# Grouping the filler work between the weighting steps of an attention and convolution kernel

## The chip, the core and the metric

The kernel runs on one core of a Trainium2 chip. The metric is the device time of one launch in microseconds (us); the time of a kernel is the median of several runs. Four engines compute: PE (TensorE, matrix multiplication into the PSUM accumulators), VectorE (DVE), ScalarE (ACT) and GpSimd (POOL). SyncE (SP) and POOL issue the DMA transfers.

## The reference

Two independent computations share one launch, and their outputs stand side by side, 640 columns each.

- A: `x` (2048 positions, 640 columns) goes through one projection to q, k and v with 32 heads of 20 columns. Each position attends to 8 earlier ones, at distances 0, 2, ... 14: `logits = q.k * scale`, softmax over the 8, `o = sum of weight * v`, and `o @ wo` is the output.
- B: for each of 640 channels a kernel `K` of length 2048 is generated from 192 complex exponentials, `u` is convolved with it by Fourier transforms, and `u * Dskip` is added.

## The kernel before

The change lies in the last stage, from about 353 us of the profiled execution on. By then all transforms of B are done but the last half of the inverse one, and the logits of A are made. What is left is done in one interleaved stream.

**The weighting (`av_step`, L600 to L623).** The 2048 positions lie as four quarters of 512 on the 128 partitions (quarter and head), so that v is a tile of 20 columns by 512 positions. For each of the 8 distances `w`, VectorE multiplies a stretch of v by the attention weights (L606, one instruction), and PE adds the product into PSUM with 16 small matmuls by an identity (32x32 tiles, tile `ps_o`), 8 for the first two quarters and 8 for the others. The products go through a ring of 6 buffers. After `w == 7` the sum is copied out of PSUM to `o` in two copies (L620, L622). Both engines go through six blocks, each of 8 steps:

- the first block: positions 0 to 255 of each quarter, columns 0 to 7 (products of 2048 columns)
- A: positions 0 to 127, columns 8 to 19 (1536)
- B: positions 128 to 255, columns 8 to 19 (1536)
- C: positions 256 to 383, columns 0 to 15 (2048)
- D: positions 256 to 511, columns 16 to 19 (1024)
- E: positions 384 to 511, columns 0 to 15 (2048)

A block takes two of three double PSUM buffers, so the second half of a block's first step waits until one copy of the block before is done. `between` is called in the middle of that step.

**The filler.** Between the steps PE does two other kinds of work:

- *Inverse parts* (`Inverse.part`, 24 of them): 12 or 8 matmuls (`ps_ib`) for 3 or 2 rows of the inverse transform, and one ScalarE copy to `ysb` (L680). Behind every third part, 8 rows are complete and SP issues four stores (L683). Six parts at a time read one of four `Z` tiles, which are loaded beforehand: the third (parts 12 to 17) and the fourth (18 to 23) in pieces during blocks A, B and C (`LOADS`, L667), the third by SP alone.
- *Output pieces* (`out_piece`, 32 of them): 5 matmuls with `wo` (`ps_op`) for half the columns of 128 positions, and a copy to `ob` (L638; for half of the last eight on VectorE, L636). Behind every second piece the 128 positions are stored. Eight pieces become possible each time that `o` is complete for a quarter of the positions: after A, B, D and E.

Both kinds, the softmax sums `ps_s` and small corrections share one pool of two single PSUM banks, so a piece waits until the piece but one before it has been copied out.

**What sets the order.** `in_order` makes matmuls, ScalarE copies and the instructions passed to `VV` keep the order of the program on their engine; other VectorE instructions may be moved by the scheduler. `fill(some, n)` takes the next n pieces from the list `parts` or `rest` and issues them. In the kernel before, one piece is issued behind nearly every step:

```
piece = lambda: fill(parts if done in (0, 2) or (done, w) == (1, 0) else rest)
att.av_step(i0, ni, j0, nj, w, done == 3, piece if w == 0 else lambda: None)
```

For positions 256 to 511 the softmax is finished during this stage: maxima and exponentials in the first block, the sums (`ps_s`) ahead of block B, and in `softmax_b` their reciprocal (L578) and the weights `atp` (L582), written behind step 3 of block B.

Of the kernel before, what the change touches and what calls it, by code (L numbers as in the profile page):

```python
# [10 lines left out]
A = mybir.AluOpType  # L11
ACT = mybir.ActivationFunctionType
AX = mybir.AxisListType
bf16 = mybir.dt.bfloat16
# [392 lines left out]
class Attention:  # L407
# [161 lines left out]
    def sums(self, hf):  # L569
        self.ps_s = self.one("ps_s")[:, 0:256]  # L570
        for w in range(W):
            self.MM(self.ps_s, lhsT=self.ident[:], rhs=self.lsb[hf][:, w], start=(w == 0), stop=(w == W - 1))

    def softmax_b(self, hf):
        nc, lsb = self.nc, self.lsb[hf]
        r = self.ta.tile([128, 256], bf16, name="recip", tag="TA0")
        with nc.allow_low_precision("weights are bf16 in the reference"):
            nc.vector.reciprocal(out=r[:], in_=self.ps_s)  # L578
        if hf == 0:
            self.AP_ = self.ta.tile([128, 4, 2048], bf16, name="atp", tag="R1")  # L580
        self.at[hf] = self.AP_[:, hf].rearrange("p (w i) -> p w i", w=W)
        nc.vector.tensor_tensor(out=self.at[hf], in0=lsb, in1=r[:].unsqueeze(1).to_broadcast([128, W, 256]), op=A.mult)  # L582

    def open_out(self, a2):
        nc = self.nc
# [103 lines left out]
def body(tc, ctx, pools, prm, B_u, B_Dskip, Sd, Zd, UDd, A_x, A_wqkv, A_wo, out_a, out_b):  # L689
    nc = tc.nc  # L690
# [13 lines left out]
    with tc.tile_pool(name="prep_b", bufs=1) as pb, tc.tile_pool(name="prep_c", bufs=1) as pc, tc.tile_pool(name="prep_a", bufs=1) as pa, tc.tile_pool(name="psum_p", bufs=2, space=bass.MemoryType.PSUM) as psp:  # L704
        pools.update(prep_a=pa, prep_b=pb, prep_c=pc)
        B, fill = partB_prep(tc, dict(pools, psum=psp), prm)
# [21 lines left out]
    att = Attention(tc, pools, A_x, A_wqkv, A_wo, out_a, psk, psg)  # L728
# [102 lines left out]
    for w in range(W):  # L831
        if w >= 2:
            att.products(1, w)
        att.logits(1, w)
        if w == 2:
            att.softmax_b(0)
        att.proj_v(2 * w)
        if w == 4:
            att.v_halo(0, 8)
# [3 lines left out]
    parts = inv.parts()  # L843
    rest = []

    def fill(some, n=1):
        for f in some[0:n]:
            f()
        del some[0:n]

    for w in range(W):
        if w < 4:
            att.proj_v1(16 + w)
        if w in (1, 4):
            att.v_halo(*((8, 8) if w == 1 else (16, 4)))
        if w >= 5:
            fill(parts)
        if w == 0:
            att.open_out(a2)
        att.av_step(0, 256, 0, 2, w)  # L860
        if w == 1:
            att.softmax_a(1)
        elif w == 3:
            att.exponentials(1)
    LOADS = {(d, w + 2 * (qr == 3)): (qr, c) for c, (d, w) in enumerate(((0, 0), (0, 4), (1, 0), (1, 4), (None, 0))) for qr in (2, 3)}
    for i0, ni, j0, nj, done in ((0, 128, 2, 3, 0), (128, 128, 2, 3, 1), (256, 128, 0, 4, None), (256, 256, 4, 1, 2), (384, 128, 0, 4, 3)):
        if done == 1:
            att.sums(1)
        for w in range(W):
            piece = lambda: fill(parts if done in (0, 2) or (done, w) == (1, 0) else rest)  # L870
            att.av_step(i0, ni, j0, nj, w, done == 3, piece if w == 0 else lambda: None)
            if done == 1 and w == 3:
                att.softmax_b(1)
            if (done, w) in LOADS:
                qr, c = LOADS[done, w]
                inv.load(qr, c, c + 1)
            if w > 0:
                piece()
            if done == 3 and w % 2 == 0:
                fill(parts)  # L880
        if done is not None:
            rest += att.out_proj(done, done == 3)
    for f in parts + rest:
# [4 lines left out]
def kernel(  # L888
# [28 lines left out]
    Zd = dpool.tile([NCH, 128, 4096], bf16, name="Zdram")  # L917
    UDd = dpool.tile([NCH, 128, 2048], bf16, name="UDdram")
    body(tc, ctx, pools, prm, B_u, B_Dskip, Sd, Zd, UDd, A_x, A_wqkv, A_wo, out_a, out_b)


# [28 lines left out]
```

## Time and profile before

| what | us |
|---|---|
| median of 3 runs | 425.13 (423.94 to 426.79) |
| the profiled execution | 420.77 |
| its span, first to last instruction | 419.0 |
| PE busy | 341.1 |
| VectorE busy | 382.7 |
| ScalarE busy | 310.5 |
| GpSimd busy | 47.9 |

The span is what the views of the trace divide up; the 1.8 us by which the execution is longer lie around it. Times in the views are counted from the start of the span. The mean granted clock of PE is 0.955 of full speed. PE's busy time is that of pipelined matmuls with modelled ends, so the time from the start of one group to the start of the next is the better measure of what it costs. In a timeline each row gives the start, the length, the engine, the line and operation, output and inputs, the number of merged instructions and, in brackets, how long the engine idled just before and what ended it. Nearly all matmuls of the last stage show L426, the helper that keeps them in order, so they are told apart by their tiles.

### The profile page before, as it was taken

What the parts mean: (1) busy time and instruction counts of PE and PEld (TensorE: products, weight loads), DVE (VectorE), ACT (ScalarE), POOL (GpSimd) and SP (SyncE); (2) the same over time, 40 slices, a digit from 0 to 9 for tenths busy, and PEclk for the clock granted to TensorE, in tenths of its full rate; (3) what the DMA queues carried; (4) which work ended last, traced back from release to release, by engine and by line L of the source; (5) the groups of instructions that cost most, each with busy time, mean ns of one, the idle gap of its engine ahead of it and who ended that gap; (6) DMA issues with size and microseconds to landing.
All of it is one profiled execution on the core that took longest, in us unless ns stands there. A gap on an engine that the chain in (4) does not pass through costs nothing.

```text
span 419.0 us, 17105 instructions
## 1 busy us (share of the span) xinstructions
PE 341.1 (81%) x7757; PEld 227.0 (54%) x7757; DVE 382.7 (91%) x381; ACT 310.5 (74%) x571; POOL 47.9 (11%) x85
## 2 busy tenths in 40 slices
PE   2375678989886887778868688999899999799996
PEld 1133463866864567455754557455555676444444
DVE  7999999999997999999999988994986899899762
ACT  3989996889999899979999492533667645754752
POOL 7540000000000000000000000170000300502110
PEclk9997598999899899989999899999999999969999
DMA  5599002164233403334029990440040292897544
GB/s 144 171 228 171 3 2 96 60 231 102 103 129 127 102 5 127 129 128 102 28 104 295 185 256 9 157 167 2 3 102 0 85 207 81 221 237 214 156 127 127
DMA packets 45129, 51.57 MB, mean 123 GB/s; under 512 B 31376, under 2 KB 38992, under 8 KB 42368
## 3 DMA queue, kind: packets, MB, share of 16 engines
q1 hardware_dynamic: 41520, 41.40, 36.7%
q0 software_dynamic: 3392, 8.95, 7.2%
q8 instruction: 61, 1.00, 1.0%
q10 hardware_dynamic: 144, 0.12, 0.1%
q14 instruction: 12, 0.10, 0.1%
HBM read 28.01 MB, written 18.35 MB: 111 GB/s over the span
## 4 chain that ended last, share of the span: by engine, by line
PE 33%; DVE 23%; ACT 19%; DMA 11%; issue 7%; SPq 6%; DVEq 0%; ACTq 0%
DVE Y L312 9%; DMA P<-Sdram 5%; ACT A L342 5%; ACT R L224 5%; PE ps_k L327 4%; PE ps_q L495 4%; PE ps_k L477 4%; PE ps_v L508 4%; PE ps_op L426 4%; DVE X L278 3%; ACT Sg L348 3%; PE ps_o L426 2%; DMA U<-in_B_u_dram 2%; DVE P L362 2%; PE ps_l L548 2%
## 5 line engine op out<-in xcount | busy, mean ns | idle before, releaser
L312 DVE TENSOR_TENSOR Y<-F,G 128x3072 bf16<-128x3072 bf16 x60 | 102.9, 1757 | 0.0
L327 PE MATMUL ps_k<-Y,X 64*32 64x64 bf16 (+1 forms) x3840 | 81.5, 237 | 20.5 <-DVE Y L312 14.5
L327 PEld LDWEIGHTS <-X 64*32 64x32 bf16 (+1 forms) x3840 | 62.2, 115 | 46.7 <-issue 32.8
L224 ACT ACTIVATE R<-LPC 128x192 bf16<-128x192 f32 x225 | 59.6, 358 | 0.1
L249 PE MATMUL ps_ph<-LPC 128*128 128x512 bf16 x100 | 32.2, 424 | 13.2 <-DMA LPC<-lo 6.2
L348 ACT CAST Sg<-ps_f 128x1024 bf16<-128x1024 f32 x40 | 37.7, 1025 | 6.1 <-PE ps_f L347 6.0
L342 ACT CAST A<-ps_f 128x1024 bf16<-128x1024 f32 x40 | 38.0, 1040 | 2.1 <-PE ps_f L341 2.0
L347 PE MATMUL ps_f<-A,T 128*128 128x128 bf16 x320 | 23.8, 235 | 16.0 <-ACT A L342 14.2
L278 DVE TENSOR_TENSOR X<-R,TX 128x1536 bf16<-128x1536 bf16 x40 | 36.5, 958 | 0.0
L261 ACT ACTIVATE TA<-ps_ph 128x1024 bf16<-128x1024 int16 (+1 forms) x40 | 30.4, 828 | 6.1 <-PE ps_ph L249 3.6
L606 DVE TENSOR_TENSOR prod<-v,atp 128x2048 bf16<-128x2048 bf16 (+2 forms) x32 | 30.8, 1018 | 2.4 <-PE ps_o L426 1.5
L347 PEld LDWEIGHTS <-T 128*128 128x128 bf16 x320 | 21.7, 106 | 17.8 <-issue 16.7
L261 ACT ACTIVATE TX<-ps_ph 128x1024 bf16<-128x1024 int16 (+1 forms) x40 | 29.6, 839 | 1.1 <-PE ps_ph L253 1.1
L537 DVE TENSOR_TENSOR prod<-qT,kT 128x1024 bf16<-128x1024 bf16 (+1 forms) x16 | 23.0, 1483 | 4.7 <-ACT qT L496 4.7
L362 DVE TENSOR_TENSOR P<-P,Sg 128x4096 bf16<-128x4096 bf16 x10 | 22.8, 2290 | 4.6 <-DMA P<-Sdram 2.6
L426 PE MATMUL ps_op<-wo,o 128*128 128x320 bf16 x160 | 26.3, 301 | 0.1
L638 ACT CAST ob<-ps_op 128x320 bf16<-128x320 f32 x28 | 12.0, 429 | 16.9 <-PE ps_op L426 15.6
L378 PE MATMUL ps_ia<-EA,P 128*128 128x128 bf16 x320 | 21.5, 220 | 2.9 <-DVE P L362 2.8
L328 ACT CAST Ksb<-ps_k 128x512 bf16<-128x512 f32 x20 | 11.7, 601 | 16.1 <-PE ps_k L327 16.0
L495 PE MATMUL ps_q<-xT,wkq 128*128 128x512 bf16 x100 | 22.6, 379 | 0.0
L477 PE MATMUL ps_k<-xT,wkq 128*128 128x512 bf16 x100 | 22.4, 379 | 0.0
L379 ACT CAST Z<-ps_ia 128x1024 bf16<-128x1024 f32 x20 | 19.4, 1014 | 3.7 <-PE ps_ia L378 3.7
(133 smaller groups left out, 601.7 us busy)
## 6 DMA issues: line engine op xcount, KB each, us to landing
Sdram<-Sg SPq DMA_DIRECT2D x5, 1024.0 KB
P<-Sdram SPq DMA_DIRECT2D x5, 1024.0 KB
P<-Sdram SPq DMA_DIRECT2D x10, 512.0 KB
Zdram<-Z SPq DMA_DIRECT2D x5, 1024.0 KB
Z<-Zdram SPq DMA_DIRECT2D x30, 128.0 KB
U<-in_B_u_dram SPq DMA_DIRECT2D x4, 640.0 KB
UDdram<-UD SPq DMA_DIRECT2D x10, 256.0 KB
out_dram<-ysb SPq DMA_DIRECT2D x32, 80.0 KB
```

The lines of the kernel that those rows point to most:

```text
L224: last = nc.scalar.activation(out=R[:, :, e, :], in_=src, func=ACT.Exp, scale=m)
L249: MM(full[:, 16 * gi:16 * gi + 16], lhsT=L[b][:, 0:128], rhs=C, start=(i == 0), stop=(i == len(ops) - 1))
L261: last = nc.scalar.activation(out=dst[:, q0:q0 + nq, 0:32, :].rearrange("p q e f -> p e q f"), in_=words.rearrange("p (e q f) -> p e q f", ...
L278: TT = lambda o, a, b, op: V.tensor_tensor(out=o, in0=a, in1=b, op=op)
L312: nc.vector.tensor_tensor(out=Y[:].rearrange("p q (b a) f -> p q b a f", a=8), in0=fa, in1=gb, op=A.mult)
L327: MM(ps[32 * g:32 * g + 32, t], lhsT=X[hb, q, 2 - k, :, f], rhs=Ys[k][hb, q, :, f], start=(t == 0 and n == 0), stop=(n == 5), tile_positio ...
L342: nc.scalar.copy(out=A1[:, :, 32 * b:32 * b + 32].rearrange("p k (j g) -> p k j g", g=4), in_=ps[:].rearrange("p j k g -> p k j g"))
L347: last = MM(ps[:, kk], lhsT=C["T2"][:, 8 * b + kk, :], rhs=A1[:, 8 * b + kk, :], start=(kk % 4 == 0), stop=True, skip_group_check=True)
L348: nc.scalar.copy(out=Sg[:, :, 8 * b:8 * b + 8, :], in_=ps[:].rearrange("p k (j g) -> p j k g", g=4))
L426: self.MM = lambda *a, **k: late(self.nc.tensor.matmul(*a, **k))
L477: MM(ps[:, i], lhsT=self.wk[:, kt, 128 * ct:128 * ct + 128], rhs=self.x4[:, kt, 2 * i:2 * i + 2, 256 * hf:256 * hf + 256], start=(kt == 0) ...
L495: MM(ps[:, i], lhsT=self.wq[:, kt, 128 * ct:128 * ct + 128], rhs=self.x4[:, kt, 2 * i:2 * i + 2, 256 * hf:256 * hf + 256], start=(kt == 0) ...
```

## The change

The filler is issued in groups, written out per block as what goes `inside` the first step and what goes `behind` which step. Mostly these are two pieces behind every second step; around the softmax sums of block B they are single. In the first block two parts behind step 6 stand for one each ahead of steps 5, 6 and 7. The number of parts or output pieces per block changes a little: first block 3 parts to 2; B 1 part and 7 output pieces to 2 and 6; D 8 parts to 6 parts and 2 output pieces; E 4 parts and 8 output pieces to 6 and 6, and one more output piece is left for behind E. The reciprocal becomes a method of its own, kept in order, and is called behind step 1 of block B; the weights `atp` are kept in order too and are written behind step 4.

```diff
+    def reciprocals(self):
+        self.r = self.ta.tile([128, 256], bf16, name="recip", tag="TA0")
+        with self.nc.allow_low_precision("weights are bf16 in the reference"):
+            self.VV(self.nc.vector.reciprocal(out=self.r[:], in_=self.ps_s))
+
     def softmax_b(self, hf):
-        nc, lsb = self.nc, self.lsb[hf]
-        r = self.ta.tile([128, 256], bf16, name="recip", tag="TA0")
-        with nc.allow_low_precision("weights are bf16 in the reference"):
-            nc.vector.reciprocal(out=r[:], in_=self.ps_s)
+        nc, lsb, r = self.nc, self.lsb[hf], self.r
...
-        nc.vector.tensor_tensor(out=self.at[hf], in0=lsb, in1=r[:].unsqueeze(1).to_broadcast([128, W, 256]), op=A.mult)
+        self.VV(nc.vector.tensor_tensor(out=self.at[hf], in0=lsb, in1=r[:].unsqueeze(1).to_broadcast([128, W, 256]), op=A.mult))
...
-        if w >= 5:
-            fill(parts)
         if w == 0:
             att.open_out(a2)
         att.av_step(0, 256, 0, 2, w)
+        if w == 6:
+            fill(parts, 2)
...
-    for i0, ni, j0, nj, done in ((0, 128, 2, 3, 0), (128, 128, 2, 3, 1), (256, 128, 0, 4, None), (256, 256, 4, 1, 2), (384, 128, 0, 4, 3)):
+    for i0, ni, j0, nj, done, inside, behind in (
+            (0, 128, 2, 3, 0, (parts, 2), {2: (parts, 2), 4: (parts, 2), 6: (parts, 2)}),
+            (128, 128, 2, 3, 1, (parts, 1), {1: (parts, 1), 2: (rest, 1), 3: (rest, 1), 4: (rest, 2), 6: (rest, 2)}),
+            (256, 128, 0, 4, None, (rest, 2), {2: (rest, 2), 4: (rest, 2), 6: (rest, 2)}),
+            (256, 256, 4, 1, 2, (rest, 2), {2: (parts, 2), 4: (parts, 2), 6: (parts, 2)}),
+            (384, 128, 0, 4, 3, (parts, 2), {2: (rest, 2), 3: (parts, 2), 4: (rest, 2), 5: (parts, 2), 6: (rest, 2)})):
...
-            piece = lambda: fill(parts if done in (0, 2) or (done, w) == (1, 0) else rest)
-            att.av_step(i0, ni, j0, nj, w, done == 3, piece if w == 0 else lambda: None)
-            if done == 1 and w == 3:
+            att.av_step(i0, ni, j0, nj, w, done == 3, (lambda: fill(*inside)) if w == 0 else lambda: None)
+            if done == 1 and w == 1:
+                att.reciprocals()
+            if done == 1 and w == 4:
                 att.softmax_b(1)
...
-            if w > 0:
-                piece()
-            if done == 3 and w % 2 == 0:
-                fill(parts)
+            if w in behind:
+                fill(*behind[w])
```

For the first half of the positions `reciprocals` is called just ahead of `softmax_b(0)`, where nothing is kept in order yet.

More of the change, by code (lines that the diff above doesn't have):

```diff
@@ L869, in body @@
         for w in range(W):
-            piece = lambda: fill(parts if done in (0, 2) or (done, w) == (1, 0) else rest)
-            att.av_step(i0, ni, j0, nj, w, done == 3, piece if w == 0 else lambda: None)
-            if done == 1 and w == 3:
+            att.av_step(i0, ni, j0, nj, w, done == 3, (lambda: fill(*inside)) if w == 0 else lambda: None)
+            if done == 1 and w == 1:
+                att.reciprocals()
+            if done == 1 and w == 4:
                 att.softmax_b(1)
```

## The prediction

> **What bounds the kernel now.** First the busy time of each engine by block, from the windows of the trace. The rows are the first block, A, B, C, D, E and the rest; the columns are the stretch, its length, busy time (instructions) of PE, its weight loads, DVE, ACT and POOL, the granted clock, the DMA share and GB/s.
>
> ```profile
> 353.53:363.75 10.22, 8.89 (x254) 4.63 (x252) 9.17 (x12) 6.54 (x11) 3.45 (x7) 1.00 0.73 206
> 363.75:373.74 9.99, 8.40 (x241) 3.90 (x217) 9.99 (x12) 7.46 (x13) 2.70 (x5) 0.75 1.08 253
> 373.74:382.79 9.05, 9.05 (x174) 4.12 (x173) 9.05 (x9) 3.55 (x8) 1.41 (x3) 0.90 0.71 190
> 382.79:392.15 9.36, 9.36 (x170) 4.35 (x169) 8.42 (x11) 4.71 (x11) 2.16 (x5) 1.00 0.77 240
> 392.15:398.00 5.85, 4.96 (x219) 2.66 (x218) 4.36 (x6) 5.16 (x11) 0.27 (x1) 1.00 0.31 90
> 398.00:407.89 9.89, 9.89 (x206) 4.67 (x204) 6.13 (x6) 5.66 (x14) 1.63 (x3) 1.00 0.53 136
> 407.89:419.00 11.11, 7.47 (x65) 4.76 (x50) 3.19 (x5) 3.65 (x8) 1.08 (x2) 1.00 0.38 120
> ```
>
> VectorE is full in A and B (9.99 of 9.99, 9.05 of 9.05) and has room in D and E (4.36 of 5.85, 6.13 of 9.89). PE is full in B, C and E; only D has a hole. So VectorE paces the start, PE the end. Next, PE's timeline, the rows with idle time from A on (in brackets), and with them the row that ends E:
>
> ```profile
> 365.06 0.52 PE L426 MATMUL ps_o<-prod,ident 32*32 32x384 bf16 x24 [0.65 <-ACT o L622]
> ...
> 366.44 0.32 PE L426 MATMUL ps_ib<-Z,HB 96*32 96x160 bf16 x8 [0.23 <-ACT ysb L680]
> ...
> 369.07 0.54 PE L426 MATMUL ps_o<-atp,ident 32*32 32x384 bf16 x14 [0.64 <-issue]
> ...
> 393.06 0.39 PE L426 MATMUL ps_ib<-Z,HB 96*32 96x160 bf16 x12 [0.61 <-DMA Z<-UDdram]
> ...
> 396.90 0.39 PE L426 MATMUL ps_ib<-Z,HB 96*32 96x160 bf16 x12 [0.28 <-ACT ysb L680]
> ...
> 407.89 7.52 PE L426 MATMUL ps_op<-wo,o 128*128 128x320 bf16 x50
> ```
>
> The wait of 0.61 in D is for the third `Z` tile. The chain of waits (start, length, what) shows what stands behind it, SP issuing stores and loads one after the other from 378.94 on until the last lands:
>
> ```profile
> 378.94 0.28 SPq L683
> ...
> 388.97 0.54 SPq L667
> ...
> 389.56 3.42 DMA Z<-UDdram
> 392.97 0.09 issue
> 393.06 0.39 PE ps_ib L426 x12
> ```
>
> So PE's lateness before D is partly free: whoever reaches the third tile's first part early waits for 392.97. What counts is the PE work that is left behind that landing.
>
> **The change part by part.**
>
> *The reciprocal* costs and gains nothing: in the two kernels as built VectorE's instructions stand in one and the same order, with the reciprocal behind step 5 of B.
>
> ```profile
> 371.92 1.89 PE L426 MATMUL ps_s<-lsb,ident 128*128 128x256 bf16 x8
> 373.74 0.52 PE L426 MATMUL ps_o<-prod,ident 32*32 32x384 bf16 x8
> 373.87 1.75 DVE L578 RECIPROCAL recip<-ps_s 128x256 bf16<-128x256 f32 x1
> ```
>
> The sums end at 373.81 and the reciprocal starts at 373.87: there is no room. But one inverse part fewer stands ahead of the sums now (10 instead of 11), so they come no later. If they did, VectorE would wait as long, in front of B's step 6; the price is bounded by what PE then still has in its ring.
>
> *First block and A.* VectorE's instructions and PE's A steps are the same. The part of 8 matmuls that completes the first 8 rows moves from ahead of step 7 to the middle of A's first step, and its ScalarE copy from before the two copies of `o` to behind them (first row: a group of such copies, count, then busy us, mean ns of one and idle time):
>
> ```profile
> L680 ACT CAST ysb<-ps_ib 128x320 bf16<-128x320 f32 x8 | 3.4, 427 | 2.7 <-PE ps_ib L426 2.5
> 362.42 1.65 ACT L680 CAST ysb<-ps_ib 128x480 bf16<-128x480 f32 x3
> 364.00 1.93 ACT L622 CAST o<-ps_o 128x1024 bf16<-128x1024 f32 x2
> ```
>
> The copies of `o` start up to 0.43 earlier, the 427 ns of that copy, and PE has two parts instead of one to fill the 0.65. Against this the pairs in A find their two banks still being copied. I take the sum of A as zero for the end, since the landing above covers it; without that cover it is worth between -1.5 (0.65, 0.23 and 0.64 gone) and +1.
>
> The first `ysb` store now starts about 1.8 later (behind 1.93 of `o`, less what moved ahead), and SP, in order, has most of its `Z` loads behind it. In the built order one load has moved ahead of it, and the stores of the third and fourth group of rows have moved behind 1 and 3 loads. SP's rows and waits here:
>
> ```profile
> 364.09 1.84 SPq L683 DMA_DIRECT2D out_dram<-ysb  x4
> ...
> SPq L683 <- ACT ysb L680: 3.9, 1, 3.9
> SPq L667 <- DMA Z<-Zdram: 0.9, 1, 0.9
> SPq L683 <- DMA Z<-Zdram: 0.5, 1, 0.5
> ```
>
> SP stood still for 3.9 ahead of 364.09, then twice for transfers in flight (0.9 and 0.5), in a stretch whose DMA share is 1.08. A later start is partly taken up there. The landing shifts by -0.5 to +1.8; I take 0.
>
> *B and C.* B has one output piece less, one part more. A pair of output pieces against two single ones:
>
> ```profile
> 385.62 0.85 PE L426 MATMUL ps_op<-wo,o 128*128 128x320 bf16 x5
> 386.40 0.43 PE L426 MATMUL ps_o<-prod,ident 32*32 32x512 bf16 x16
> ```
>
> A piece takes 386.40 - 385.62 = 0.78. In the row of 50 at 407.89 ten pieces one after another take 7.52, or 0.75 each. So each pair saves about 0.04. [...] These rows show no more than that. B and C change by -0.5 in PE time, which the landing covers too.
>
> *D.* At its first step two output pieces (1.53) stand where one part stood, and the first part on the third tile comes behind step 2 instead of in the middle of step 0. It needs the tile 1.53 + 2.5 steps later; a step of D is 394.38 - 394.12 = 0.26:
>
> ```profile
> 393.80 0.39 PE L426 MATMUL ps_ib<-Z,HB 96*32 96x160 bf16 x12
> 394.12 0.33 PE L426 MATMUL ps_o<-prod,ident 32*32 32x256 bf16 x16
> 394.38 0.32 PE L426 MATMUL ps_ib<-Z,HB 96*32 96x160 bf16 x8
> ```
>
> That is 2.2 later. PE came to it at about 392.45 before; it would now come at about 394.6, or up to 1.5 sooner by the gains in A, B and C. So the 0.61 goes, and the landing has between 0 and 1.6 of slack.
>
> *D and E behind the landing.* Before, PE took from 393.06 to 407.89 = 14.83: 12 parts, 7.5 steps of D, 8 of E and 7 output pieces (the eighth stands behind E's last step). After, there are 12 parts, 5 steps of D, 8 of E and 6 output pieces. That is 2.5 x 0.26 = 0.65 and 0.78 less. With three pairs of output pieces (0.12) and the 0.28 of 396.90 gone, it is 1.83 less. New waits stand against it. A pair needs both banks at once, while ScalarE copies in order:
>
> ```profile
> 391.48 1.93 ACT L622 CAST o<-ps_o 128x1024 bf16<-128x1024 f32 x2
> ...
> 395.33 1.52 ACT L680 CAST ysb<-ps_ib 128x480 bf16<-128x480 f32 x3 [0.15 <-PE ps_ib L426]
> ...
> 397.80 1.08 ACT L622 CAST o<-ps_o 128x512 bf16<-128x512 f32 x2
> ```
>
> At E's first step the copy of D's `o` (half of 1.08) comes behind a part's copy (1.52 / 3 = 0.51), and two parts (0.32 each, 394.12 - 393.80) cover 0.64 of it: about 0.2 is left. Two steps on, the pair of output pieces needs the banks of those two parts, copied behind all of the 1.08: about 0.2 again. In D the pairs of parts come every 0.26 x 2 + 0.64 = 1.16, and ScalarE needs 1.02 for two: it keeps up, barely. New waits: 0.4 to 2.6 (the upper end if each of the six pairs of parts in D and E waits one 0.43). I take 0.9, nearer to the rows that I can follow.
>
> *Behind E* nothing changes: in both kernels two old output pieces and then the eight last ones follow E's last step.
>
> **The sum:** -1.83 + 0.9 = -0.93 behind the landing, 0 at the landing, 0 for the rest. The profiled execution goes from 420.77 to 419.8 (span 418.0). The median of the runs shown stands 4.36 above that execution, so on the median's scale it is 425.13 - 0.93 = 424.2.
>
> **The rivals.**
>
> *No bound moves* (the regrouping does nothing): the gains are small against 425, and the new waits may equal 1.83. Time 425.1.
>
> *SP is the bound, and slower:* the first store is 1.8 late, nothing is taken up, and the third tile lands at 394.8. From a landing later than 392.97 + 0.93 = 393.9 the change loses; at 1.8 it is +0.87, 426.0. For it: SP issues without a break from 378.94 to 390. Against it: the load that moved ahead, and the 0.9 and 0.5.
>
> [...]
>
> *The clock.* PE's clock falls to half in A:
>
> ```profile
> 368.00:369.00 1.00, 0.43 (x14) 0.09 (x3) 1.00 (x2) 0.70 (x2) 0.00 (x0) 0.86 1.15 298
> 369.00:370.00 1.00, 0.93 (x38) 0.35 (x37) 1.00 (x2) 0.00 (x0) 0.00 (x0) 0.50 1.18 287
> ...
> 375.00:376.00 1.00, 1.00 (x29) 0.42 (x5) 1.00 (x2) 0.12 (x1) 0.00 (x0) 0.73 0.72 199
> 324.97 1.03 PE L572 MATMUL ps_s<-ql,ident 128*128 128x256 bf16 x8 [0.24 <-ACT ql L567]
> ```
>
> It lasts from about 368.7 to 375.5 (0.86 and 0.73 are means of a full and a half part). The sums take 1.89 in it and 1.03 at 324.97, at full clock. If such a stretch of 6.8 fell into E, where nothing covers it, half of it would be lost: +3.4, 427.6. If it went away, A and B would gain about 2, and the landing would cover most of that: 423. [...]
>
> *More than forecast:* the third tile lands up to 0.5 sooner, nothing waits at the banks, 0.4 is left of the new waits: 425.13 - 1.83 + 0.4 - 0.5 = 423.2; with the idle rows of A gone and the landing sooner still, 421.5.
>
> **How the numbers follow.** Chances: forecast (423.4 to 424.8) 0.40; no bound moves 0.16; SP 0.12; banks 0.10; clock 0.08; more than forecast 0.14. The predicted time is that of the likeliest, 424.2. The range takes in the clock's 427.6 above and the last case's 421.5 below; with some 0.5 on each side for the spread of the runs shown (423.94 to 426.79) it is 421.0 to 428.0. A per cent is 4.25, which is about what a measurement of this kernel can tell from no change. No term worked out here reaches it alone: the largest is the clock's 3.4. Faster by over 1% asks for the last case together with the clock's gain, or for a cause that no row shows: 0.11, out of the last case and the clock's. Slower by over 1% asks for two of the slower cases at once (the clock with the banks or with SP), or again for an unseen cause: 0.11, out of those three. Within 1% is 0.78.
>
> **What would show it.** Right: in D no idle time of PE for `Z`, or one of under 0.3; the stretch from the landing to the end of E about 13.9 instead of 14.83; the waits of `ps_ib` and `ps_op` for ScalarE's copies some 0.9 more in D and E; the ten pieces behind E as long as before; VectorE without a wait in A and B. Wrong: a landing of the third tile beyond 394; waits for `ysb` copies at every pair; a half-clock stretch in D or E; a fall of the chain back to VectorE, with PE waiting for products.

## The result and the profile after

The changed kernel takes 420.83 us (median of 22 executions, 417.56 to 426.42) against 424.02 for the kernel before on the same chips (22 executions, 419.34 to 427.72). The ratio is 0.9944, with a 95% interval of 0.9916 to 0.9971: 2.4 us faster, between 1.2 and 3.6. It leaves out the slow executions, those over 1.5% above the fastest of their kernel, and so it is not the quotient of the two medians. The forecast was 0.93 faster.

The profile that came with the result is of an execution with a low clock (0.911, span 423.6), so the kernel before is compared with a second profile of the same changed kernel (span 416.6, clock 0.950); the first one is read further down for what it alone shows.

The windows by block of that second profile, with the same columns as those of before: first block, A, B, C, D, E, rest. Each window begins at the first matmul of its block. The first window of before begins 1.18 ahead of that matmul (354.71), so its first block takes 9.04 counted this way.

```profile
353.74:362.14 8.40, 7.20 (x224) 3.98 (x228) 7.32 (x9) 5.02 (x10) 2.82 (x5) 1.00 0.69 188
362.14:372.30 10.16, 8.18 (x272) 4.39 (x256) 10.16 (x13) 7.40 (x14) 3.31 (x7) 0.83 0.96 242
372.30:381.92 9.62, 8.23 (x159) 4.01 (x143) 9.62 (x10) 3.14 (x8) 1.13 (x2) 0.82 0.69 184
381.92:390.29 8.37, 8.37 (x184) 4.55 (x168) 7.73 (x10) 4.62 (x11) 2.17 (x4) 1.00 0.86 261
390.29:395.79 5.50, 5.13 (x218) 3.01 (x202) 4.13 (x5) 5.10 (x10) 1.08 (x2) 1.00 0.47 162
395.79:405.56 9.77, 9.34 (x238) 5.11 (x229) 6.93 (x7) 6.62 (x16) 1.08 (x2) 1.00 0.60 146
405.56:416.60 11.04, 7.46 (x66) 4.78 (x50) 3.19 (x5) 3.60 (x8) 1.08 (x2) 0.96 0.34 111
```

The first block, A and B together take 28.18 against 28.08 before (382.79 less 354.71): VectorE is full in A and B again. C takes 8.37 against 9.36, D 5.50 against 5.85, E 9.77 against 9.89, the rest 11.04 against 11.11. So the stage from C to E takes 23.64 against 25.10, which is 1.46 less, and two thirds of that (0.99) come from C.

C has the same work in both kernels: 8 steps and 8 output pieces, PE busy without a break. PE's timeline shows why it is shorter. Of the kernel before, the row behind the step at 386.40:

```profile
386.77 0.85 PE L426 MATMUL ps_op<-wo,o 128*128 128x320 bf16 x5
```

and of the changed kernel, a pair of output pieces, the two steps behind it and the next pair:

```profile
384.51 1.53 PE L426 MATMUL ps_op<-wo,o 128*128 128x320 bf16 x10
385.97 0.65 PE L426 MATMUL ps_o<-prod,ident 32*32 32x512 bf16 x32
386.56 1.53 PE L426 MATMUL ps_op<-wo,o 128*128 128x320 bf16 x10
```

Before, a piece takes 0.78 (385.62 to 386.40) and a step 0.37 (386.40 to 386.77). Two of each are 2.30. Now the pair takes 1.46 (384.51 to 385.97) and the two steps 0.59 (385.97 to 386.56), together 2.05. That is 0.25 per pair: 0.10 on the pieces and 0.15 on the steps. Four pairs are 1.00, and C is 0.99 shorter.

In D and E the timeline of the changed kernel shows:

```profile
390.51 1.53 PE L426 MATMUL ps_op<-wo,o 128*128 128x320 bf16 x10
391.98 0.65 PE L426 MATMUL ps_o<-prod,ident 32*32 32x256 bf16 x40
392.86 0.72 PE L426 MATMUL ps_ib<-Z,HB 96*32 96x160 bf16 x24 [0.23 <-DMA Z<-UDdram]
393.51 0.33 PE L426 MATMUL ps_o<-prod,ident 32*32 32x256 bf16 x16
393.63 0.32 PE L426 MATMUL ps_o<-atp,ident 32*32 32x256 bf16 x16
393.91 0.85 PE L426 MATMUL ps_ib<-Z,HB 96*32 96x160 bf16 x20
...
396.82 0.53 PE L426 MATMUL ps_ib<-Z,HB 96*32 96x160 bf16 x19 [0.24 <-issue]
...
405.56 1.53 PE L426 MATMUL ps_op<-wo,o 128*128 128x320 bf16 x10
```

The two output pieces stand where PE stood idle before, and two steps of D side by side take 0.40 (393.51 to 393.91) instead of 2 x 0.26. From the first part on the third tile to the end of E it is now 405.56 - 392.86 = 12.70 instead of 14.83. The idle rows are 0.23 and 0.24 (0.61 and 0.28 before).

One wait is new. PE's timeline of the changed kernel in B:

```profile
374.68 1.44 PE L426 MATMUL ps_op<-wo,o 128*128 128x320 bf16 x5 [1.18 <-DVE recip L577]
```

The first output piece takes the PSUM bank in which the softmax sums stand, and this is free only when the reciprocal has read them. Counted from the first matmul of the stage, the sums now end at 17.86 instead of 19.10, while VectorE begins the reciprocal when it did before (19.14 and 19.16), so PE is there too early.

The first profile, with the low clock, shows another course (a row of PE's timeline in D, then one pair of output pieces in E and what follows it):

```profile
396.68 0.75 PE L426 MATMUL ps_ib<-Z,HB 96*32 96x160 bf16 x24 [1.92 <-DMA Z<-Zdram]
...
403.20 2.85 PE L426 MATMUL ps_op<-wo,o 128*128 128x320 bf16 x10
405.97 0.65 PE L426 MATMUL ps_o<-atp,ident 32*32 32x512 bf16 x16
```

and, in windows of its last stage (the clock is the first of the last three columns):

```profile
396.00:397.00 1.00, 0.32 (x20) 0.35 (x24) 0.91 (x1) 0.00 (x0) 0.10 (x1) 0.99 0.80 288
397.00:398.00 1.00, 1.00 (x53) 0.36 (x46) 0.09 (x1) 0.88 (x2) 0.00 (x0) 0.50 0.18 64
...
406.00:407.00 1.00, 1.00 (x33) 0.56 (x36) 0.00 (x0) 0.43 (x1) 0.15 (x1) 0.50 0.00 0
407.00:408.00 1.00, 1.00 (x35) 0.47 (x24) 0.00 (x0) 0.94 (x2) 0.40 (x1) 0.89 0.08 31
```

Here the third tile landed 39.28 after the first matmul of the stage, hardly later than in the second profile (39.11), but PE was at D 1.47 earlier (35.08 after that matmul instead of 36.55). So it stood still for 1.92. Right behind that its clock fell to half, from about 397.0 to 407.2. The pair of output pieces takes 2.77 instead of 1.46, and C to E take 28.33 in place of 23.64.

### The profile page after: what moved, and what is told of

Read it like the earlier page. It is cut to its first block, busy times and chain, and to the rows that moved or that the text cites. A ratio compares the mean times of both kernels' runs of the same rounds, so it can differ in the third digit from the quotient of the medians.

```text
span 423.6 us, 17104 instructions
## 1 busy us (share of the span) xinstructions
PE 347.7 (82%) x7757; PEld 233.9 (55%) x7757; DVE 382.3 (90%) x381; ACT 310.6 (73%) x571; POOL 48.4 (11%) x85
## 4 chain that ended last, share of the span: by engine, by line
PE 36%; DVE 24%; ACT 20%; issue 7%; DMA 7%; SPq 5%; DVEq 0%; ACTq 0%
DVE Y L312 8%; PE ps_k L327 7%; ACT R L224 5%; ACT A L342 5%; PE ps_q L495 4%; ACT Sg L348 4%; PE ps_k L477 4%; PE ps_v L508 4%; PE ps_op L426 4%; DVE X L278 3%; DMA U<-in_B_u_dram 2%; PE ps_l L548 2%; ACT Z L379 2%; PE ps_o L426 2%; SPq L170 2%
## 5 line engine op out<-in xcount | busy, mean ns | idle before, releaser
L249 PE MATMUL ps_ph<-LPC 128*128 128x512 bf16 x100 | 34.7, 452 | 11.3 <-DMA BD<-c_BD 6.2
L347 PE MATMUL ps_f<-A,T 128*128 128x128 bf16 x320 | 27.5, 259 | 14.9 <-ACT A L342 13.8
L347 PEld LDWEIGHTS <-T 128*128 128x128 bf16 x320 | 25.4, 119 | 16.5 <-issue 15.6
L341 PE MATMUL ps_f<-BD,U 128*64 128x128 bf16 x320 | 19.7, 284 | 3.3 <-ACT Z L379 3.1
```

What stands on the lines that cost most here:

```text
L249: MM(full[:, 16 * gi:16 * gi + 16], lhsT=L[b][:, 0:128], rhs=C, start=(i == 0), stop=(i == len(ops) - 1))
L347: last = MM(ps[:, kk], lhsT=C["T2"][:, 8 * b + kk, :], rhs=A1[:, 8 * b + kk, :], start=(kk % 4 == 0), stop=True, skip_group_check=True)
```

## The experiments

The table puts all profiles side by side: the lengths of C, D and E (from the first matmul of a block to that of the next; E up to the row of the last pieces), PE's idle time in D, the granted clock of D and E, and the ratio to the kernel before with its interval (12 executions of the kernel named, 11 for e2, 6 for e7, 22 for the result, against 22 to 35 of the kernel before). Apart from the ratio, each line is one profiled execution.

| kernel | C | D | E | C to E | idle in D | clock D, E | ratio |
|---|---|---|---|---|---|---|---|
| before | 9.36 | 5.85 | 9.89 | 25.10 | 0.89 | 1.00, 1.00 | |
| changed, low clock | 8.37 | 7.87 | 12.09 | 28.33 | 1.92 | 0.79, 0.71 | 0.9944 (0.9916 to 0.9971) |
| e1 changed again | 8.37 | 5.50 | 9.77 | 23.64 | 0.37 | 1.00, 1.00 | 0.9938 (0.9893 to 0.9984) |
| e2 front only | 8.37 | 7.55 | 12.21 | 28.13 | 1.15 | 0.69, 0.78 | 1.0103 (1.0062 to 1.0144) |
| e3 tail only | 9.37 | 4.98 | 9.74 | 24.09 | 0.61 | 1.00, 1.00 | 0.9947 (0.9907 to 0.9988) |
| e4 third tile first | 8.37 | 5.51 | 9.87 | 23.75 | 0.37 | 1.00, 1.00 | 0.9927 (0.9879 to 0.9975) |
| e5 pins alone | 9.36 | 5.66 | 9.98 | 25.00 | 0.92 | 1.00, 1.00 | 1.0019 (0.9973 to 1.0064) |
| e6 before, third tile first | 9.37 | 5.90 | 9.94 | 25.21 | 1.13 | 1.00, 1.00 | 0.9987 (0.9946 to 1.0029) |
| e7 e4, earlier reciprocal | 8.37 | 5.50 | 9.57 | 23.44 | 0.37 | 1.00, 1.00 | 0.9890 (0.9821 to 0.9958) |
| e8 e4, no pieces in D | 8.37 | 7.06 | 12.10 | 27.53 | 2.17 | 0.86, 0.80 | 1.0020 (0.9980 to 1.0060) |
| e9 moved, single | 8.44 | 5.98 | 10.37 | 24.79 | 0.37 | 1.00, 1.00 | 0.9998 (0.9951 to 1.0044) |
| e10 e6, copy on VectorE | 9.37 | 5.06 | 10.02 | 24.45 | 0.44 | 1.00, 1.00 | 0.9961 (0.9924 to 0.9999) |
| e11 e8, copy on VectorE | 8.37 | 8.58 | 11.23 | 28.18 | 4.21 | 0.96, 0.88 | 0.9983 (0.9938 to 1.0028) |
| e12 e7, copy on VectorE | 8.37 | 5.28 | 9.64 | 23.29 | 0.24 | 1.00, 1.00 | 0.9963 (0.9924 to 1.0002) |

Two readings stand in the columns. C is 8.37 in all eight profiles with pairs in C, and 9.36 or 9.37 in all five with eight single pieces (e9 has seven). And D and E are at full clock in the ten lines with up to 1.13 idle in D, and below it in the four with 1.15 or more.

**e1, the changed kernel again.** No edit.

> The changed kernel once more, for a profile with the usual clock. Theory L (the landing of the third Z tile sets when PE goes on in block D, and the gain is the work left behind it): PE waits 0.5 to 2 us for Z in D, the time from the first ps_o to the last row of output pieces is 52 to 53 us against 53.2 before, ratio to before 0.993 to 0.998. Rival P (pairs of pieces make PE itself shorter): no wait for Z in D above 0.3 us, same ratio.

Measured 0.9938 (0.9893 to 0.9984), which repeats the result; its profile is the second one above. From the first matmul of the stage to the last pieces it takes 51.82 (53.18 before), less than theory L had, and it waits 0.23 for `Z`, as rival P had it.

**e2 and e3, one end each.** In e2 the first block, A, B and C are grouped, D and E as before:

```diff
-            (256, 256, 4, 1, 2, (rest, 2), {2: (parts, 2), 4: (parts, 2), 6: (parts, 2)}),
-            (384, 128, 0, 4, 3, (parts, 2), {2: (rest, 2), 3: (parts, 2), 4: (rest, 2), 5: (parts, 2), 6: (rest, 2)})):
+            (256, 256, 4, 1, 2, (parts, 1), {v: (parts, 1) for v in range(1, 8)}),
+            (384, 128, 0, 4, 3, (rest, 1), {v: (rest, 1) for v in range(1, 8)})):
...
+            if done == 3 and w % 2 == 0:
+                fill(parts)
```

e3 is the reverse: D and E from the changed kernel, the blocks ahead of them with single pieces.

> First block, A, B and C grouped as in the change; D and E one piece at a time as before. Theory L: PE reaches D earlier but needs the third tile in the middle of D's first step, so the wait for Z grows from 0.61 to 1.5 to 2.5 us and the time is that of before, ratio 0.999 to 1.003. Rival P: two thirds of the pairs are here, so two thirds of the gain, ratio 0.995 to 0.997.

> First block, A, B and C one piece at a time as before; D and E grouped as in the change (one output piece stands inside D's first step, since only one is left). Theory L: the wait for Z in D goes away or stays under 0.6 us, most of the gain is here, ratio 0.994 to 0.998. Rival P: a third of the gain, ratio 0.998 to 0.999.

e2 is slower, 1.0103 (1.0062 to 1.0144), which neither of its expectations had. e3 is at 0.9947 (0.9907 to 0.9988), in theory L's range, and can't be told from the whole change. The windows of C, D and E, first of e2:

```profile
385.17:393.54 8.37, 8.37 (x184) 4.56 (x168) 7.34 (x9) 4.62 (x11) 2.17 (x4) 1.00 0.83 248
393.54:401.09 7.55, 6.40 (x232) 2.98 (x208) 6.54 (x8) 5.86 (x11) 0.54 (x1) 0.69 0.34 92
401.09:413.30 12.21, 12.21 (x208) 5.07 (x204) 4.61 (x4) 5.62 (x14) 1.62 (x3) 0.78 0.32 82
```

then of e3:

```profile
383.70:393.07 9.37, 9.37 (x170) 4.36 (x169) 9.18 (x11) 4.71 (x11) 2.17 (x5) 1.00 0.79 240
393.07:398.05 4.98, 4.37 (x198) 2.61 (x205) 3.71 (x6) 4.17 (x9) 0.81 (x2) 1.00 0.51 154
398.05:407.79 9.74, 9.35 (x239) 5.12 (x230) 6.78 (x6) 6.63 (x16) 1.08 (x2) 1.00 0.55 134
```

In e2 C wins its 0.99, and D and E give it back and more: holes of 0.53 and 0.39 for ScalarE's copies, then a stretch at half clock; besides, an eleventh output piece is left behind E (0.75), since B has issued one piece less. The low clock is not that one profile's alone: the granted clock of the whole span averages 0.917 over e2's 11 executions and 0.930 over 34 of the kernel before. In e3 D and E take 14.72 against 15.74 before, with the same 12 parts and 7 output pieces in them; two parts of D and one output piece of E have changed places. So e3 shows a gain in D and E that doesn't need the front. Its one wait ahead of a part on the third tile (0.39) is for ScalarE's copy to `ob` and not for `Z`. What a pair of parts or pieces is worth, e2's D and E can't say, since half clock lies over them.

**e5, the reciprocal and the pins alone,** all pieces single as before:

> Only the reciprocal of its own and the pins, filler as before; every engine's instructions stand in the order of the kernel before. Theory L: nothing, ratio 0.997 to 1.003, and the profile is a second one of the order before: from the first ps_o to the last ten output pieces 53.2 us unless PE's clock falls elsewhere. Rival C (a half-clock stretch in D and E is common in the order before, and the change makes it rarer): a half-clock stretch in D or E, 55 us or more.

Measured 1.0019 (0.9973 to 1.0064), C to E 25.00 against 25.10. VectorE, ScalarE and GpSimd run their instructions in the order of before, and PE does in this stage. So the reciprocal part is worth nothing by itself, and the profile is a second one of the order before.

**e4 and e6, the third tile's loads ahead of the fourth's,** on the changed kernel (e4) and on the kernel before (e6):

```diff
-    LOADS = {(d, w + 2 * (qr == 3)): (qr, c) for c, (d, w) in enumerate(((0, 0), (0, 4), (1, 0), (1, 4), (None, 0))) for qr in (2, 3)}
+    SLOTS = [(d, w) for d in (0, 1) for w in (0, 2, 4, 6)] + [(None, 0), (None, 2)]
+    LOADS = {s: (2 + n // NCH, n % NCH) for n, s in enumerate(SLOTS)}
```

> The changed kernel with the loads of the third Z tile all ahead of those of the fourth, in the same places. Theory L: the third tile lands some 5 us earlier, the wait for Z in D is gone and the kernel is 0.5 to 2 us faster than the changed one, ratio to before 0.988 to 0.993, unless the fourth tile is late in E. Rival P: nothing moves, ratio as the changed kernel's, 0.994.

> The kernel before with the loads of the third Z tile ahead of those of the fourth. Theory L: the wait of 0.61 in D goes, 0.3 to 0.6 us, ratio 0.998 to 1.000. Rival C: the hole in D is what lets the clock fall; without it the time falls by 2 to 3 us, ratio 0.993 to 0.996.

Measured 0.9927 (0.9879 to 0.9975) for e4, which e1 can't be told from, and 0.9987 (0.9946 to 1.0029) for e6. PE's idle row of e4 in D, where e1 has 0.23 for `Z`:

```profile
390.51 0.72 PE L426 MATMUL ps_ib<-Z,HB 96*32 96x160 bf16 x24 [0.23 <-ACT ob L640]
```

and the two of e6, where before has 0.61 for `Z` and 0.28:

```profile
396.80 0.39 PE L426 MATMUL ps_ib<-Z,HB 96*32 96x160 bf16 x12 [0.69 <-ACT ob L638]
...
400.06 0.39 PE L426 MATMUL ps_ib<-Z,HB 96*32 96x160 bf16 x12 [0.44 <-ACT ysb L680]
```

The tile comes earlier and a wait stays, now for ScalarE's copies. In e6 it stands ahead of D's second part, which begins 1.65 after D does. Before, the second part began at the same place (393.80 less 392.15), just behind the end of that copy (393.29 and 0.46 make 393.75), and the wait for `Z` ahead of the first part filled the time. The copy in ScalarE's timeline of the kernel before:

```profile
393.29 0.46 ACT L638 CAST ob<-ps_op 128x320 bf16<-128x320 f32 x1
```

e5 shows this without any change to the loads. With the order of before, but the tile there in time, its wait in D is ScalarE's, and its second part too begins 1.65 after D (396.06):

```profile
397.71 0.39 PE L426 MATMUL ps_ib<-Z,HB 96*32 96x160 bf16 x12 [0.69 <-ACT ob L640]
```

So behind the landing on which the prediction put the wait there stood a second reason of about the same length: the second part needs a bank that ScalarE empties only behind its copies of C's `o`. The early tile can still be worth something in other executions: in e4's profile PE is at D as early (35.18) as in the low-clock profile of the changed kernel, and waits 0.23 instead of 1.92.

**e10, e6 with the second copy of C's `o` on VectorE:**

```diff
-            att.av_step(i0, ni, j0, nj, w, done == 3, piece if w == 0 else lambda: None)
+            att.av_step(i0, ni, j0, nj, w, done in (None, 3), piece if w == 0 else lambda: None)
```

> The kernel before with the loads of the third tile first, and the second copy of C's o on VectorE instead of ScalarE. Theory S: ScalarE is free 0.97 earlier in D, the wait of 0.69 there shrinks to under 0.3, D shorter by 0.4 to 0.9, ratio 0.997 to 0.999. Rival: the wait in D is not ScalarE's and stays at 0.6 to 0.7, ratio as with the loads alone, 0.999.

Measured 0.9961 (0.9924 to 0.9999). Of the two idle rows of e6 one is left:

```profile
397.74 0.39 PE L426 MATMUL ps_ib<-Z,HB 96*32 96x160 bf16 x12 [0.44 <-ACT ysb L680]
```

D takes 5.06 instead of 5.90 with the same work, and its second part begins 0.89 after D instead of 1.65. This shows that ScalarE paced D in e6, and, by the same 1.65, in the kernel before. The change reaches the same place otherwise: two output pieces stand where the parts waited.

**e9, pieces moved but not paired.** C issues seven output pieces instead of eight, so that two are left for D's first two steps; D has 6 parts and E 6 parts and 6 output pieces, all single. The first block, A and B are as before:

```diff
...
+            (256, 128, 0, 4, None, (rest, 1), {v: (rest, 1) for v in range(1, 7)}),
+            (256, 256, 4, 1, 2, (rest, 1), {1: (rest, 1), **{v: (parts, 1) for v in range(2, 8)}}),
+            (384, 128, 0, 4, 3, (parts, 1), {v: (rest, 1) for v in range(1, 7)})):
...
+            if done == 3 and w in (0, 2, 4, 5, 6):
+                fill(parts)
```

> No pairs at all: one piece at a time as before, but two output pieces are kept back from C for D's first two steps, D has 6 parts, E 6 parts and 6 output pieces, two are left behind E. Theory S (ScalarE's copies pace D, and the gain is the output pieces that PE does there in time that was idle): the whole gain, ratio 0.993 to 0.997, 51.5 to 52.5 us from the first ps_o to the last ten output pieces, D+E 15.3 us against 15.74. Rival P (the pairs are the gain): ratio 0.999 to 1.001.

Measured 0.9998 (0.9951 to 1.0044), as rival P had it. But the interval still overlaps that of the change (0.9916 to 0.9971), so the division rests on the windows of C, D and E:

```profile
383.23:391.67 8.44, 8.44 (x165) 3.97 (x171) 7.50 (x9) 3.79 (x10) 1.90 (x4) 1.00 0.78 243
391.67:397.65 5.98, 5.61 (x219) 2.93 (x195) 4.98 (x6) 5.39 (x10) 1.08 (x2) 1.00 0.38 129
397.65:408.02 10.37, 9.99 (x226) 4.69 (x223) 6.09 (x6) 6.36 (x16) 1.08 (x2) 1.00 0.52 127
```

Moving fills D's holes (0.37 idle instead of 0.89) and is worth 25.10 - 24.79 = 0.31 from C to E. The other 1.15 of the change's 1.46 come only with the pairs, and e1 even has one output piece more in these blocks (16 instead of 15), which B gave up. D and E alone hold the same parts and pieces in e9 and in e1. They take 16.35 and 15.27, with PE idle for 0.75 and 0.80, so the 1.08 between them is PE's own time, with pairs and without. C of e9 agrees: with one piece and one change of tiles less than before it is 0.92 shorter, 0.14 more than a piece takes.

**e8 and e11, pairs without output pieces in D,** both on e4's loads; e11 also has the copy of e10:

```diff
-            (256, 256, 4, 1, 2, (rest, 2), {2: (parts, 2), 4: (parts, 2), 6: (parts, 2)}),
-            (384, 128, 0, 4, 3, (parts, 2), {2: (rest, 2), 3: (parts, 2), 4: (rest, 2), 5: (parts, 2), 6: (rest, 2)})):
+            (256, 256, 4, 1, 2, (parts, 2), {2: (parts, 2), 4: (parts, 2), 6: (parts, 2)}),
+            (384, 128, 0, 4, 3, (rest, 2), {1: (parts, 2), 2: (rest, 2), 3: (parts, 2), 4: (rest, 2), 6: (rest, 2)})):
```

> The changed kernel with the loads of the third tile first, but with 8 parts in pairs and no output piece in D; the two output pieces stand in E's first step. Theory L with the tile landed: what the output pieces covered in D's first step, the copy of o, shows as a wait of 0.3 to 0.6 us, nothing else, ratio 0.993 to 0.996. Rival C: without the dense pieces the clock falls in D or E, ratio 0.998 or more and a half-clock stretch in the profile.

> The kernel without output pieces in D (third tile's loads first), with the second copy of C's o on VectorE. If ScalarE's backlog makes the holes of D and these let the clock fall: waits in D 2.0 us before, under 1 now, no half-clock stretch in D and E, ratio 0.994 to 0.998. If the holes do not matter for the clock: the stretch of 7 us or more stays, ratio 0.999 to 1.003.

Measured 1.0020 (0.9980 to 1.0060) and 0.9983 (0.9938 to 1.0028): the gain is lost in e8, as rival C had it, and e11 can be told neither from no change nor from e8. PE's idle rows of e8 in D:

```profile
393.09 0.65 PE L426 MATMUL ps_o<-prod,ident 32*32 32x256 bf16 x40 [0.51 <-ACT o L624]
394.47 0.86 PE L426 MATMUL ps_ib<-Z,HB 96*32 96x160 bf16 x20 [0.73 <-ACT ysb L682]
...
397.13 0.99 PE L426 MATMUL ps_ib<-Z,HB 96*32 96x160 bf16 x24 [0.46 <-ACT ysb L682]
```

Pairs of parts alone do wait for copies to `ysb` at the banks in D (0.73 and 0.46); with two output pieces there they don't (e4's only idle row in D is its 0.23 for `ob`). The half clock of e8's profile is not shown to be what loses the gain: the granted clock of the whole span averages 0.929 over its 12 executions, as over e4's 12. In e11 these waits for `ysb` are gone, but the parts of the fourth tile come earlier there, and one wait of 3.68 stands in front of them that the trace puts down to a transfer. So e11 doesn't separate what it was made for.

**e7 and e12, for a faster version.** e7 is e4 with B's products kept in order (by `pin`, which in `av_step` is laid around the product) and the reciprocal behind B's step 3; e12 adds the copy of e10:

```diff
-    def av_step(self, i0, ni, j0, nj, w, vec=False, between=lambda: None):
+    def av_step(self, i0, ni, j0, nj, w, vec=False, between=lambda: None, pin=lambda ins: ins):
...
-            att.av_step(i0, ni, j0, nj, w, done == 3, (lambda: fill(*inside)) if w == 0 else lambda: None)
-            if done == 1 and w == 1:
+            att.av_step(i0, ni, j0, nj, w, done == 3, (lambda: fill(*inside)) if w == 0 else lambda: None, *((att.VV,) if done == 1 else ()))
+            if done == 1 and w == 3:
                 att.reciprocals()
```

> The changed kernel with the loads of the third tile first and VectorE's reciprocal behind step 3 of B instead of step 5 (its products of B kept in order). Theory: PE's new wait for the reciprocal in B (0.6 to 1.9 us) shrinks to under 0.5 us, and with the landing out of the way 0.3 to 1 us of it reaches the end: ratio 0.989 to 0.992. Rival: VectorE paces B and C anyway, ratio as with the loads alone, 0.993.

> The changed kernel with the third tile's loads first, the reciprocal behind step 3 and the second copy of C's o on VectorE. Theory S: D's waits are only 0.23 and 0.30 with the output pieces there, so the copy is worth 0 to 0.4: ratio 0.987 to 0.991. If VectorE's 1.2 us copy delays D's products instead: 0.990 to 0.993.

Measured 0.9890 (0.9821 to 0.9958) and 0.9963 (0.9924 to 1.0002). PE's new wait for the reciprocal is gone in both profiles, but e4's profile, without this edit, has none either, so that is not shown to be the edit's doing alone. VectorE, which paces B (9.62 of 9.62 busy in e1), starts the reciprocal 1.0 sooner in e7 than in e1 (18.14 after the first matmul of the stage instead of 19.14), and now waits for the sums ahead of it (0.65, and 0.74 in e12). C to E take 23.44 and 23.29, close to e1's 23.64. Neither is shown to beat the changed kernel: the intervals overlap, and e12, with everything e7 has, lies nearer to 1 than either of its expectations.

## Why the prediction came out as it did

The direction was right, and the time stayed within one per cent, as was thought likeliest. The gain was more than forecast (0.93; measured 2.4, between 1.2 and 3.6). On the prediction's scale 0.9944 of 425.13 is 422.75, which lies not in the forecast's 423.4 to 424.8 but in the case *more than forecast*; the interval, 421.6 to 423.9, reaches into both. Of the reasons given for that case one held (hardly a wait at the banks) and one did not (a landing up to 0.5 sooner). By the prediction's steps:

- *What paces what.* Right for the front: the first block to the start of C takes 27.2 to 29.0 in the six kernels with single pieces there and 26.7 to 29.4 in the eight with groups, so nothing that was moved there is seen. E is PE's, as said. Wrong for D: the 0.61 was not the landing's alone. In e5 and e6 the tile was there in time and 0.69 stayed; e10 took the copy away and it went.
- *The reciprocal costs nothing.* Right in time (e5). That no wait comes of it was wrong: PE waits for its bank in B in most profiles of the changed order there (0.55 in the first profile of the change, 1.18 in e1, 1.85 in e2; none in e4). VectorE, which paces B, is busy all through it (9.62 of 9.62 in e1).
- *A pair saves 0.04.* **This is the step that failed by its size.** The prediction took the piece in a row of ten (0.75) against a piece between steps (0.78) and left the steps out. Measured: 0.25 per pair, 0.15 of it on the two steps that now stand side by side. In C alone this is 0.99, where the prediction's 0.04 for each of four pairs is 0.16.
- *The landing covers what the blocks ahead of it gain.* Wrong in e1, where the landing costs 0.23, which e4 spends on ScalarE with the tile there early. Right in the low-clock profile: there PE was at D 1.47 earlier and the landing took it all back.
- *The landing shifts by -0.5 to +1.8, taken as 0.* It fell inside: counted from the first matmul of the stage it came 0.85 later in e1 (392.85 less 353.74, against 392.97 less 354.71). In the low-clock profile it came at 396.62, 1.02 later than before. The rival of SP priced a landing 1.8 later, which neither profile shows; that the landing cost 1.92 there is mostly PE's being early.
- *Behind the landing: -1.83 of work and +0.9 of waits.* Measured -2.13 (12.70 instead of 14.83). The work was right but for the steps side by side; of the waits only one of 0.24 is seen, for which the trace names no cause. (The first "about 0.2" among them comes to 0.4 by its own figures: 0.54 and 0.51 of copies less 0.64.) The banks, to which the chances give 0.10, did not come to the 2.6 of six pairs of parts waiting 0.43 each in the changed kernel, but e8 shows such waits: 0.73 and 0.46 for `ysb`, once the two output pieces of D no longer give ScalarE time. The prediction had allowed for that wait everywhere and missed that the two pieces prevent it. In its own terms e1 is 0.77 later at the landing (first part at 39.12 instead of 38.35) and 2.13 shorter behind it, 1.36 in sum. The forecast's 0 and 0.93 erred both ways, so that 0.93 comes near to it is in part luck.
- *Behind E nothing changes.* Right: 11.04 against 11.11.
- *The clock as a rival, 3.4 if a stretch falls in D or E.* It does in one of the two profiles of the changed kernel, and with the wait of 1.92 ahead of it C to E are 4.7 longer. PE's busy time from C to E grows by 3.5 (26.32 against 22.84). That this is close to 3.4 is luck: the stretch is 10.2 long and not 6.8, and costs a third of its length and not half. How often it happens in the changed kernel and in the one before is not known, since each run gives one profile. The granted clock of the whole span, which is on record for more executions, shows no difference: it averages 0.927 over 22 of the changed kernel, and 0.930, 0.928 and 0.926 in three sets of 34, 29 and 35 of the kernel before.

Of its own signs, the wait for `Z` in D (0.23) and the ten last pieces (7.46 and 7.52) came as named for a right prediction. The way from the landing to the end of E did not (12.70, not about 13.9), and a half-clock stretch in D and E, named as a sign of being wrong, shows in one of two profiles.

The sum at full clock is -1.46 from C to E, inside the measured interval of -1.2 to -3.6. Whether the rest of 2.4 is spread, or fewer stretches at half clock, of which the averages above show no sign, stays open.

## What to carry to other kernels

When two kinds of matmul of different tile size alternate, price both sides of the change: measure a whole round (piece and step) and not the piece alone, since here 0.15 of the 0.25 per pair was on the small matmuls that came to stand side by side. A wait that the trace puts down to a transfer can have a second reason of the same length behind it (here 0.61 for `Z`, and 0.69 for ScalarE's copy once the tile was there); move the transfer and look again before anything is covered by it. Pairs in a shared pool of two banks want work of another kind ahead of them while the copying engine is behind, as the two output pieces in D show against e8 (0.73 and 0.46 for `ysb`, in e4 only 0.23, for `ob`).

## What the runs showed of the hardware

In C the alternation itself has a price. One round from 128x128 to 32x32 tiles and back less saves 0.25 at full clock (2.05 instead of 2.30), with PE busy on both sides. What the 0.25 is made of, no run here separates.

The half clock in D and E came only behind holes in D: the four profiles with 1.15 to 4.21 us of idle time there have it, the ten with 0.24 to 1.13 don't. That is no threshold: in e2 the clock fell when 1.03 of its 1.15 had passed, and in e6 it stayed up at 1.13. It is an association over one profile of each kernel; the averages over all executions set e2 apart (0.917), but not e8 and e11 (0.929 and 0.930). Nor is the length of a single hole what these profiles share: the clock fell in the microsecond behind a hole of 1.92 in the low-clock profile of the changed kernel and behind one of 3.68 in e11, and the longest hole ahead of the fall is 0.53 in D of e2, 0.73 in D of e8 and 0.65 in A of the kernel before.
